# Attention over selected key blocks and a two-layer GELU: other products in the second layer, and one score scheme for all batches

## The chip, the cores and the metric

The kernel runs on one core of one Trainium2 chip. The metric is the device time of one execution in microseconds. Of 8 executions the median was 269.89 us (268.59 to 277.04). One execution was profiled: it took 270.17 us, of which the span from the first to the last instruction is 268.5 us, at a mean granted TensorE clock of 0.991.

A core has five engines, each with its own queue that runs in order: TensorE (PE), VectorE (DVE), ScalarE (ACT), GpSimd (POOL) and SyncE (SP, which here only issues transfers). TensorE multiplies a stationary operand, loaded first (PEld), with a moving one, and adds into PSUM. DVE and ACT read PSUM; all but TensorE write SBUF.

## The reference

There are 4 batches, 8 heads, 768 positions and 64 channels a head. Keys are taken in 12 blocks of 64. Each query scores the mean key of each block (the gate), keeps its top 3 causal blocks and its own block, and attends to those positions that are not after it.

```python
k_rep = k.reshape(B, H, n_blocks, block, D).mean(axis=3)
gate_scores = np.einsum('bhsd,bhnd->bhsn', q, k_rep)
causal = pos[:, None] // block >= np.arange(n_blocks)[None, :]
gate_scores = np.where(causal, gate_scores, -1000000000.0)
top_idx = np.argsort(gate_scores, axis=-1)[..., -top_k:]
...
sel = set(top_idx[b, h, i].tolist()) | {own_block[i]}
...
mask = mask & (pos[:, None] >= pos[None, :])
scores = np.where(mask, scale * np.matmul(q, k.transpose(0, 1, 3, 2)), -1000000000.0)
attn = softmax(scores)
attn_out = np.matmul(attn, v)
```

The heads of a token are laid side by side as x, 3072 rows of 512. Two layers follow, with `w_in` 512 by 2048 and `w_out` 2048 by 512:

```python
h = x @ w_in
g = gelu_tanh(h)
out = g @ w_out
```

Inputs and output are in fp32; the kernel multiplies in fp16.

## The kernel before

**Order of the work.** The code does not issue its instructions directly. `add(...)` records an operation: the engines that may run it with an estimated time on each, what it depends on, a priority, and the buffers that it takes and gives back. `Plan.solve` (lines 53 to 129) runs a list schedule over these estimates, picks an engine where there is a choice, hands out PSUM and other buffers, and sorts the operations by planned start. The instructions are then issued in that order, so each engine's queue is the planned one. On the chip a late operation holds up those behind it on its engine.

PSUM is shared in two groups (line 221). Two tiles `wide` of two banks each serve the scores and the first layer. Four tiles `bank` of one bank each serve `pre` (gates, transposes; at most 3), `pv` (sums of probabilities times values; at most 2) and `ops` (second layer; at most 2, in the last batch all 4).

**Stages.** Work goes by batch, and within a batch by pair `p` of heads (4 pairs a batch, 16 in all; `hp` is the pair within its batch and `i = p % 4` the set of buffers).

- `pre(p)` turns q and k so that channels lie on partitions, both heads above one another (rows 0 to 63 and 64 to 127), casts them to fp16, computes gates on TensorE and the choice of blocks on DVE, and lays the choice out as a mask of 12 rows a head. Batch 0 turns by TensorE; batches 1 to 3 by DVE (L418), from loads in 32 by 32 blocks.
- Scores come with keys on partitions and queries as columns, so that the exponentials are already the stationary operand of the product with the values. Only key chunks that are not after the queries are computed.
- The exponential is one ACT instruction a unit; GpSimd zeroes the half of the diagonal chunks that is after the query (affine select); the product with the values carries a column of ones that gives the sum of the row; DVE normalises (`norm2`, `norm`) and `turn_out` transposes the result into xT.
- `s1(b)` is the first layer with the GELU on ACT (L938, L950). Its result G is held in four quarters, A11, A12, A21, A22: even or odd chunk of 128 hidden units, first or second half of the batch's queries.
- `s2_plain(0)` is the second layer of batch 0 as it stands (L1025). `s2(b)` for batches 1 to 3 uses seven products of quarters in place of eight. The second layer of a batch is interleaved by the plan with the attention of the next batch.

**Two score schemes.** In batch 0, `heads2` (lines 674 to 783) works on both heads at once. A unit is a list of (key chunk, first query, number of queries). For each part, four matmuls are issued: q and k of head 0 on rows 0 to 63, of head 1 on rows 64 to 127, then the mask `mT2` against the constant `E2` in the same way, added into the same columns. Each uses 64 of TensorE's 128 rows. A unit has up to 512 columns a head. The data live in `kT2`, `qT2` and `mT2`, which lie inside the buffers `XS` of the second layer's sums; `E2` lies inside G.

In batches 1 to 3, `heads` (lines 845 to 922) works head by head. `kT16[i][h]` and `qT16[i][h]` hold 64 rows of data and, below them, 12 rows of mask and of the constant, so that one matmul of 76 rows gives masked scores. A unit is two key chunks, 896 columns, three matmuls (two in the last group). Two heads make six units a pair. The lower rows of `kT16` are filled once from E2 by eight small transfers on SP (`fill`, L375); the mask rows of `qT16` by copies from PSUM (batch 1) or from a transposing transfer into `mT` (batches 2 and 3).

**The second layer in seven products.** `FACT` (line 971) lists the two factors of each product. `w_sums` makes five sums of quarters of `w_out` (in two halves of the hidden units), `sums(b, c)` five sums of quarters of G for each of four chunks of a batch; three go to XS, two replace A21 and A12. `token(t)` (three a batch) runs the seven products into two banks, P and Q. Each `half` is one product: 8 matmuls of 256 columns into one half of a bank. P takes products 3 and 4, Q 1 and 6; both are copied out whole (ACT or DVE), DVE adds three times between the copied quarters (L1123), P takes 5 and 2 and is copied again, DVE subtracts it (L1138), and 7 is added at the end from Q (L1145).

Fillers (`warm`, L1174) are matmuls without use that the plan sets where TensorE would be idle.

Of the kernel before, what the change touches and what calls it, by code (L numbers as in the profile page):

```python
# [132 lines left out]
def kernel(  # L133
# [60 lines left out]
    for i in range(NK):  # L194
# [5 lines left out]
          for x in range(3)]  # L200
# [3 lines left out]
    kT2, qT2, mT2 = [[XS[x][:, 2 * i:2 * i + 2, :].rearrange("p a b -> p (a b)")  # L204
                      for i in range(HP)] for x in range(3)]
    E2 = G[:, 1, 1, NJ - 2:NJ, :].rearrange("p a b -> p (a b)")
# [5 lines left out]
    qT16, kT16, v16, madd = [], [], [], []  # L212
    for i in range(NB):
        qT16.append([persist.tile([128, S], FP16, name=f"qT_{i}_{h}")
                     for h in range(2)])
        kT16.append([persist.tile([128, S], FP16, name=f"kT_{i}_{h}")
                     for h in range(2)])
        v16.append(persist.tile([128, NC, 2, 65], FP16, name=f"v_{i}"))
        madd.append(persist.tile([128, NG, 64], FP16, name=f"madd_{i}"))
# [111 lines left out]
    def consts():  # L331
# [31 lines left out]
        for i in range(NB):  # L363
            def emit_p(_, i=i):
                nc.gpsimd.memset(v16[i][:, :, :, 64:65], 1.0)
                nc.gpsimd.memset(madd[i], 0.0)
                nc.gpsimd.memset(mT2[i][:, 0:128], 0.0)
                for h in range(2):
                    nc.gpsimd.memset(qT16[i][h][64:76, 0:128], 0.0)
            c_E["ones", i] = add({POOL: 1.1}, emit_p, [], prio=-45 + 10 * i)  # L370

    def fill(i):
        def emit(_):
            for h in range(2):
                nc.sync.dma_start(out=kT16[i][h][64:76, :], in_=E2[0:12])  # L375
        go = add({SP: 1.1}, emit, [c_E["E"], issued["v", 3]], 45 + i, lag=3.0)
        c_E["fill", i] = add({"NONE": 0.0}, lambda _: None, [go], 45)

    groups = [(0, 5), (1, 4), (2, 3)]
    last = {}  # L380

    def pre(p):
# [69 lines left out]
        else:  # L452
# [12 lines left out]
            def kc_all(h):  # L465
                def emit(eng):
                    copy(eng, kT16[i][h][0:64, :],
                         T["kT32", p][64 * h:64 * h + 64, :])
                return emit
            kcs = [add({DVE: 0.56, POOL: 0.85}, kc_all(h),  # L470
                       [t, old.get("k", None)], pr + 0.1) for h in range(2)]

# [104 lines left out]
        else:  # L577
            def q16(h):
                def emit(eng):
                    copy(eng, qT16[i][h][0:64, :],  # L580
                         T["qT32", p][h * 64:(h + 1) * 64, :])
                return emit
            q16s = [add({DVE: 0.56, ACT: 0.84}, q16(h), qcs + [old.get("s")],
                        pr + 0.1) for h in range(2)]
# [9 lines left out]
        def mask_dma(_):  # L594
            T["mT", p] = hd2.tile([128, S - 128], FP16, tag="mT",
                                 name=f"mT_{p}")
            nc.sync.dma_start_transpose(
                out=T["mT", p].rearrange("p (c q) -> p c q", q=128),
                in_=madd[i].rearrange("p g n -> p (g n)"))
# [19 lines left out]
        else:  # L619
            byPE = p < 2 * HP  # L620
            if byPE:
                m = add({PE: 0.3}, mask, [sel], pr, takes=("pre", ("mk", p, 0)))
            else:
                go = add({SP: 1.3}, mask_dma, [sel], -50)
                m = add({"DMA": 0.8}, lambda _: None, [go], pr, lag=6.0)

            def mc(h):
                def emit(eng):
                    src = (plan.buf["mk", p, 0].bitcast(FP16)[:, 128:S] if byPE
                           else T["mT", p])  # L630
                    copy(eng, qT16[i][h][64:76, 128:S],
                         src[64 * h:64 * h + 12, :])
                return emit
            mcs = [add({DVE: 0.5, ACT: 0.7} if byPE else {DVE: 0.33}, mc(h),
                       [m, old.get("s")], pr) for h in range(2)]
            if byPE:
                add({"NONE": 0.0}, lambda _: None, mcs, pr,
                    gives=[("mk", p, 0)])
            rdy[p] = [kcs[0::2] + [q16s[0], mcs[0], c_E["fill", i]],
                      kcs[1::2] + [q16s[1], mcs[1], c_E["fill", i]]]  # L640
# [33 lines left out]
    def heads2(p):  # L674
        i = p % NB
        base = 100 * p
        pvs = [[], []]
        for ui, unit in enumerate(units(p)):
# [4 lines left out]
            def st_e(_, u=u, unit=unit):  # L683
                st = plan.buf[("st",) + u]
                col = 0
                for jc, q0, w in unit:
                    for src, msk in ((kT2[i], False), (E2, True)):
                        mov = mT2[i] if msk else qT2[i]
                        for h in range(2):
                            nc.tensor.matmul(  # L690
                                st[:, 512 * h + col:512 * h + col + w],
                                src[64 * h:64 * h + 64,
                                    jc * 128:jc * 128 + 128],
                                mov[64 * h:64 * h + 64, q0:q0 + w],
                                start=not msk, stop=msk,
# [3 lines left out]
            st = add({PE: n * 2 / 2400 + 0.01}, st_e, rdy[p][late], pr,  # L699
                     takes=("wide", ("st",) + u))  # L700

            def ex_e(_, u=u, n=n):
# [8 lines left out]
                     [st, table(("exp", 0), [], base)], pr,  # L711
                     takes=("at", ("at", u)), gives=[("st",) + u])
            exps.setdefault(0, []).append(ex)
# [69 lines left out]
        last.setdefault(p, {}).update({"v": pvs[1][-1]})  # L783

    def norm(p, h):
        def emit(_):
            pvv = plan.buf["pv", p, h][:, 0:NC * 66].rearrange(
                "p (c w) -> p c w", w=66)
            if ("xn", p) not in T:
                T["xn", p] = hd.tile([128, NC, 2, 64], FP16, tag="xn",  # L790
                                     name=f"xn_{p}")
            zr = hd.tile([128, NC, 1], FP32, tag="zr", name=f"zr_{p}_{h}")
            nc.vector.reciprocal(out=zr, in_=pvv[:, :, 64:65])
            nc.vector.tensor_tensor(  # L794
                out=T["xn", p][:, :, h, :], in0=pvv[:, :, 0:64],
                in1=zr.to_broadcast([128, NC, 64]), op=ALU.mult)
        return emit

    def turn_out(p, norms, base):
# [28 lines left out]
        elif p == HP - 1:  # L828
# [15 lines left out]

    def heads(p):
        b, hp = divmod(p, HP)
        i = p % NB
        base = 1000 * b + 100 * hp
        norms = []
        for h in range(2):  # L850
            pvs = []
            for gi, (ja, jb) in enumerate(groups):
                u = (p, h, gi)
                pr = base + 10 * (3 * h + gi)
                wa = S - ja * 128
                wb = S - jb * 128

                def st_e(_, u=u, ja=ja, jb=jb, wa=wa, wb=wb, h=h):
                    st = plan.buf[("st",) + u]
                    for jc, cb in ((ja, 0), (jb, wa)):  # L860
                        s0 = jc * 128
                        w = S - s0
                        x = cb
                        while x < cb + w:
                            e = min(cb + w, (x // 512 + 1) * 512)
                            nc.tensor.matmul(  # L866
                                st[:, x:e], kT16[i][h][0:76, s0:s0 + 128],
                                qT16[i][h][0:76,
                                           s0 + (x - cb):s0 + (e - cb)],
                                start=True, stop=True)  # L870
                            x = e
                st = add({PE: 0.39}, st_e,
                         rdy[p][h] + [s1_mm[b - 1][2 * NJ - 2]], pr,
                         takes=("wide", ("st",) + u))

                def ex_e(_, u=u, n=wa + wb):
                    T["at", u] = atp.tile([128, 896], FP16, tag="at",
                                          name="at_%d_%d_%d" % u)
                    nc.scalar.activation(  # L879
                        out=T["at", u][:, 0:n],  # L880
                        in_=plan.buf[("st",) + u][:, 0:n],
                        func=AF.Exp, bias=0.0, scale=SCALE)
                ex = add({ACT: 0.84}, ex_e,
                         [st, table(("exp", b), list(gelus.get(b - 1, {}).values()), base)],
                         pr, takes=("at", ("at", u)),
                         gives=[("st",) + u])
                exps.setdefault(b, []).append(ex)

                def af_e(_, u=u, wa=wa):
                    at = T["at", u]  # L890
                    dg = bass.AP(at.tensor, at.offset,
                                 [at.ap[0], [wa, 2], [1, 128]])
                    nc.gpsimd.affine_select(  # L893
# [121 lines left out]
    def quads(x, diag):  # L1015
        return bass.AP(x.tensor, x.offset + (0 if diag else HD),
                       [x.ap[0], [3 * HD if diag else HD, 2], [1, HD]])
# [248 lines left out]
```

## Time and profile before

| what | us |
|---|---|
| median of 8 executions | 269.89 (268.59 to 277.04) |
| the profiled execution | 270.17 |
| its span | 268.5 |
| first layer, L938, 512 matmuls, busy | 85.2 |
| second layer with seven products, L1075, busy | 64.0 |
| second layer of batch 0, L1025, busy | 26.3 |
| scores of batches 1 to 3, L866, 192 matmuls, busy | 39.5 |
| scores of batch 0, L690, 192 matmuls, busy | 12.7 |
| probabilities times values, L905 and L754 | 27.3 and 8.6 |
| exponentials of batches 1 to 3, L879, 72 at 917 ns | 61.5 |
| exponentials of batch 0, L705, 24 at 917 ns | 21.4 |
| sums of quarters of G, L1009, 60 on DVE | 34.1 |
| sums of quarters of w_out, L991, 10 on DVE | 7.0 |

Busy times of matmuls overlap one another, since one starts before the one before it has ended; the distance from start to start says how long TensorE was taken. The stages lie one behind the other: attention of batch 0 up to 43.6 us, first layer of batch 0 to 65, attention of batch 1 with the second layer of batch 0 to 105.2, first layer of batch 1 to 127.9, attention of batch 2 with the second layer of batch 1 to 168.7, first layer of batch 2 to 191.4, attention of batch 3 with the second layer of batch 2 to 225.0, first layer of batch 3 to 245.7, and its second layer to the end.

### The profile page before, as it was taken

Reading aid. Unit: us, or ns where it says so; the run is one execution under the profiler, and the core shown is the slowest. Engines: PE = TensorE matmul, PEld = TensorE weight load, DVE = VectorE, ACT = ScalarE, POOL = GpSimd, SP = SyncE. Lnnn points to the kernel's source line nnn. Section 1 sums busy time; section 2 is a strip of 40 time slices with the busy share of each in tenths; the row PEclk is TensorE's granted clock in tenths of the full one; section 3 lists DMA queues with packets and bytes.
Section 4 is the critical chain, followed back from the end, with each engine's and each line's share of the span. In section 5 each row is a group of like instructions: output and inputs, shape, how many; then the busy total and the mean of one; then the engine's idle time right before and its main releaser. Section 6 shows DMA issues by size and latency. Waiting matters only on the chain.

```text
span 268.5 us, 6581 instructions
## 1 busy us (share of the span) xinstructions
PE 257.5 (96%) x2542; PEld 178.1 (66%) x2542; DVE 189.5 (71%) x554; ACT 173.6 (65%) x221; POOL 85.2 (32%) x165
## 2 busy tenths in 40 slices
PE   6999999999998999999897999999999999999993
PEld 5777777565555665555565788565777797567882
DVE  1777745713589999989998999999965463335532
ACT  2268688557968984667894975456799943665221
POOL 8557734001455461320283652020045400000000
PEclk9999999999999999999997999999999999999999
DMA  8996898999898969998894394231103312000222
GB/s 163 218 212 133 152 207 120 185 196 181 165 190 151 206 148 177 192 163 156 131 177 90 57 202 139 89 40 24 27 1 110 61 67 94 0 0 2 78 79 80
DMA packets 130816, 32.63 MB, mean 122 GB/s; under 512 B 124544, under 2 KB 126688, under 8 KB 130784
## 3 DMA queue, kind: packets, MB, share of 16 engines
q1 hardware_dynamic: 126048, 27.62, 51.4%
q0 software_dynamic: 3136, 4.19, 9.7%
q10 hardware_dynamic: 1600, 0.39, 0.7%
q8 instruction: 20, 0.33, 0.5%
q14 instruction: 12, 0.10, 0.1%
HBM read 27.26 MB, written 6.29 MB: 125 GB/s over the span
## 4 chain that ended last, share of the span: by engine, by line
PE 68%; DVE 17%; ACT 4%; SPq 3%; issue 2%; DMA 2%; POOL 2%; DVEq 0%; ACTq 0%; POOLq 0%
PE wide L938 23%; PE bank L1075 18%; PE wide L866 4%; PE wide L690 4%; PE bank L1174 3%; PE bank L1025 3%; PE bank L905 3%; ACT at L879 3%; DVE XS L1009 3%; SPq L263 2%; PE bank L754 2%; PE bank L398 2%; DVE qT L236 2%; PE bank L517 2%; DVE qT L418 2%
## 5 line engine op out<-in xcount | busy, mean ns | idle before, releaser
L938 PE MATMUL wide<-xT,w_in 128*128 128x384 f16 x512 | 85.2, 326 | 0.0
L950 ACT ACTIVATE G<-wide 128x768 f16<-128x768 f32 x64 | 51.9, 811 | 35.5 <-PE wide L938 35.0
L938 PEld LDWEIGHTS <-w_in 128*128 128x128 f16 x512 | 49.4, 98 | 33.4 <-issue 1.8
L879 ACT ACTIVATE at<-wide 128x896 f16<-128x896 f32 x72 | 61.5, 917 | 8.5 <-PE wide L866 4.6
L893 POOL TENSOR_SCALAR_AFFINE_SELECT at<-at 128x256 f16<-128x256 f16 x72 | 33.8, 473 | 61.4 <-ACT at L879 60.1
L866 PE MATMUL wide<-qT,kT 76*128 76x512 f16 (+1 forms) x192 | 39.5, 310 | 0.8 <-ACT at L879 0.7
L1075 PEld LDWEIGHTS <-G 128*128 128x128 f16 x288 | 27.6, 98 | 5.2 <-issue 1.0
L905 PEld LDWEIGHTS <-at 128*128 128x128 f16 x504 | 23.9, 99 | 10.5 <-POOL at L893 3.7
L1009 DVE TENSOR_TENSOR XS<-G 128x768 f16<-128x768 f16 x36 | 21.0, 619 | 13.7 <-ACT G L950 13.6
L905 PE MATMUL bank<-v,at 128*128 128x65 f16 x504 | 27.3, 197 | 2.5 <-DVE xn L794 1.8
L232 ACT COPY osb<-bank 128x512 f32<-128x512 f32 x23 | 13.5, 586 | 23.2 <-PE bank L1075 20.0
L705 ACT ACTIVATE at<-wide 128x1024 f16<-128x1024 f32 (+3 forms) x24 | 21.4, 917 | 9.2 <-PE wide L690 8.0
L1025 PE MATMUL bank<-w_out,G 128*128 128x512 f16 x96 | 26.3, 379 | 0.6 <-DVE xn L794 0.6
L866 PEld LDWEIGHTS <-kT 76*128 76x128 f16 x192 | 15.9, 99 | 11.0 <-issue 2.5
L1075 PEld LDWEIGHTS <-XS 128*128 128x128 f16 x216 | 20.5, 98 | 3.1
L234 POOL CAST v<-v_sd 128x768 f16<-128x768 f32 x13 | 11.8, 905 | 29.5 <-DMA v_sd<-in_v_dram 28.8
L234 POOL CAST kT<-kT 64x768 f16<-64x768 f32 x17 | 14.0, 822 | 21.9 <-DVE kT L418 21.6
L1075 PE MATMUL bank<-TS,G 128*128 128x256 f16 x144 | 20.4, 275 | 0.0
L1075 PE MATMUL bank<-w_out,G 128*128 128x256 f16 x144 | 19.8, 272 | 0.4 <-DVE w_out L991 0.4
L1075 PE MATMUL bank<-w_out,XS 128*128 128x256 f16 x144 | 19.5, 272 | 0.0
L1123 DVE TENSOR_TENSOR osb<-osb 128x256 f32<-128x256 f32 x27 | 11.7, 434 | 9.2 <-ACT osb L232 8.6
L418 DVE STREAM_TRANSPOSE kT<-k_sd 128x768 f32<-128x768 f32 x12 | 11.6, 970 | 6.1 <-DMA k_sd<-in_k_dram 6.0
(95 smaller groups left out, 345.7 us busy)
## 6 DMA issues: line engine op xcount, KB each, us to landing
out_dram<-osb SPq DMA_DIRECT2D x24, 256.0 KB
v_sd<-in_v_dram SPq DMA_DIRECT2D x26, 192.0 KB
k_sd<-in_k_dram SPq DMA_DIRECT2D x48, 96.0 KB
q_sd<-in_q_dram SPq DMA_DIRECT2D x48, 96.0 KB
w_in<-in_moe_w_in_dram POOLq DMA_DIRECT2D x2, 1024.0 KB, 11.4
w_out<-in_moe_w_out_dram POOLq DMA_DIRECT2D x2, 1024.0 KB, 12.3
G<-in_k_dram SPq DMA_DIRECT2D x4, 192.0 KB
G<-in_q_dram SPq DMA_DIRECT2D x4, 192.0 KB
```

Of the source, the lines that this page charges most:

```text
L234: nc.gpsimd.tensor_copy(out=out, in_=in_)
L418: nc.vector.transpose(out=T[key + "T32", p], in_=T[key, p].rearrange("p t j -> p (t j)"))
L705: nc.scalar.activation(out=T["at", u][:, :, 0:n], in_=plan.buf[("st",) + u].rearrange("p (h w) -> p h w", h=2)[:, :, 0:n], func=AF.Exp, bi ...
L866: nc.tensor.matmul(st[:, x:e], kT16[i][h][0:76, s0:s0 + 128], qT16[i][h][0:76, s0 + (x - cb):s0 + (e - cb)], start=True, stop=True)
L879: nc.scalar.activation(out=T["at", u][:, 0:n], in_=plan.buf[("st",) + u][:, 0:n], func=AF.Exp, bias=0.0, scale=SCALE)
L893: nc.gpsimd.affine_select(out=dg, in_=dg, compare_op=ALU.is_ge, fill=0.0, base=0, pattern=[[0, 2], [1, 128]], channel_multiplier=-1)
L905: nc.tensor.matmul(pvv[:, qc, 0:65], at[:, cb + (qc - jc) * 128: cb + (qc - jc + 1) * 128], v16[i][:, jc, h, :], start=(gi == 0 and jc == ...
L938: nc.tensor.matmul(hps[:, 512 * e:512 * e + HALF], w_in16[:, ci, (2 * j + e) * 128: (2 * j + e + 1) * 128], T["xT", b][:, ci, HALF * h:HAL ...
L950: nc.scalar.activation(out=G[:, :, h, j, :], in_=plan.buf["hps", b, j, h].rearrange("p (e w) -> p e w", e=2)[:, :, 0:HALF], func=AF.Gelu_a ...
L1009: nc.vector.tensor_tensor(out=dst[:, js], in0=i0[:, js], in1=i1[:, js], op=op)
L1025: nc.tensor.matmul(plan.buf["ops", b, ti], G[:, f % 2, 2 * ti // NC, f // 2, ti % (NC // 2) * 128:ti % (NC // 2) * 128 + 128], w_out16[:, ...
L1075: nc.tensor.matmul(dst[:, HD * h:HD * h + HD], FACT[m][0][:, j, t * 128:(t + 1) * 128], FACT[m][1][:, j, :], start=(first and j == 0 and h ...
```

## The change

**Scores.** `heads` and all that it needs go (`kT16`, `qT16`, `fill`, `norm`, `mT`). All batches use `heads2`. `kT2`, `qT2`, `mT2` become buffers of their own, one set for each `i`, and so does `E2`. In batches 1 to 3 the casts of q and k are one copy of 128 rows each instead of two of 64, with POOL allowed for q as well; the mask is one copy from PSUM in batch 1, and in batches 2 and 3 the transposing transfer writes `mT2` without a copy behind it. All of these wait for the last scores of the pair that used the buffers before.

Queries up to 191 have at most three causal blocks, so all of them are selected, and the first 64 queries of a diagonal chunk see their own block alone. The mask matmul of a part now starts at `max(q0, 192, jc * 128 + 64)`, and is left out where nothing remains. This holds in batch 0 too.

**Second layer.** The seven products are formed from four sums of each factor, each made from the one before. Products 1, 2 take raw quarters of both factors, 3 raw weights, 4 and 7 a raw or replaced quarter of G. One quarter of G is replaced instead of two, and one of `w_out`. In `token` the order is 1 and 5 into P, 2 and 6 into Q, 3 onto 5 in P, 4 over 1 in P, 7 onto 6 in Q. One half of a bank is copied; the other steps are DVE adds that read PSUM directly.

The last pair of every batch is turned by TensorE in two halves, as was done in batch 0 alone.

```diff
-    kT2, qT2, mT2 = [[XS[x][:, 2 * i:2 * i + 2, :].rearrange("p a b -> p (a b)")
-                      for i in range(HP)] for x in range(3)]
-    E2 = G[:, 1, 1, NJ - 2:NJ, :].rearrange("p a b -> p (a b)")
+    kT2, qT2, mT2 = [[persist.tile([128, S], FP16, name=f"{x}T2_{i}")
+                      for i in range(NB)] for x in "kqm"]
+    E2 = persist.tile([128, S], FP16, name="E2")
...
-            kcs = [add({DVE: 0.56, POOL: 0.85}, kc_all(h),
-                       [t, old.get("k", None)], pr + 0.1) for h in range(2)]
+            kcs = [add({DVE: 0.56, POOL: 0.85},
+                       lambda eng: copy(eng, kT2[i], T["kT32", p]),
+                       [t, old.get("s")], pr + 0.1)]
...
+            q16s = [add({DVE: 0.56, ACT: 0.84, POOL: 0.85},
+                        lambda eng: copy(eng, qT2[i], T["qT32", p]),
+                        qcs + [old.get("s")], pr + 0.1)]
...
-                go = add({SP: 1.3}, mask_dma, [sel], -50)
-                m = add({"DMA": 0.8}, lambda _: None, [go], pr, lag=6.0)
+                go = add({SP: 1.3}, mask_dma, [sel, old.get("s")], -50)
+                mcs = [add({"DMA": 0.8}, lambda _: None, [go], pr, lag=6.0)]
...
+                    q1 = max(q0, 192, jc * 128 + 64)
+                    for src, mov, lo in ((kT2[i], qT2[i], q0),
+                                         (E2, mT2[i], q1)):
+                        if lo >= q0 + w:
+                            continue
...
-            st = add({PE: n * 2 / 2400 + 0.01}, st_e, rdy[p][late], pr,
-                     takes=("wide", ("st",) + u))
+            cols = n + sum(max(0, q0 + w - max(q0, 192, jc * 128 + 64))
+                           for jc, q0, w in unit)
+            st = add({PE: cols / 2400 + 0.01}, st_e,
+                     rdy[p][late] + ([s1_mm[b - 1][2 * NJ - 2]] if b else []),
+                     pr, takes=("wide", ("st",) + u))
...
-    def heads(p):
...
-    FACT = {1: (XS[0], TS[:, 0]), 2: (XS[1], B11), 3: (A11, B12),
-            4: (A22, B21), 5: (XS[2], B22), 6: (A21, TS[:, 1]),
-            7: (A12, TS[:, 2])}
+    FACT = {1: (A11, B11), 2: (A12, B21), 3: (XS[2], B22),
+            4: (A22, TS[:, 2]), 5: (XS[0], TS[:, 0]), 6: (XS[1], TS[:, 1]),
+            7: (A21, B12)}
...
+                    (5, TS[:, 0], B12, B11, ALU.subtract),
+                    (6, TS[:, 1], B22, TS[:, 0], ALU.subtract),
+                    (7, B12, B22, B12, ALU.subtract),
+                    (4, TS[:, 2], B21, TS[:, 1], ALU.subtract)):
...
+                (5, XS[0], A21, A22, ALU.add),
+                (6, XS[1], XS[0], A11, ALU.subtract),
+                (3, XS[2], A12, XS[1], ALU.subtract),
+                (7, A21, A11, A21, ALU.subtract)):
...
+            half(1, "P", 1, True, [])
+            mm = half(5, "P", 0, False, [])
+            ao = add({DVE: 0.36, ACT: 0.4}, a_e, [mm], post,
+                     takes=("osb", ("osb", key)))
+            eo = add({DVE: 0.34}, join(
+                lambda: quad(3), lambda: two(bank_of("P")[:, 0:HD]),
+                lambda: quad(2)), [ao], post)
+            half(2, "Q", 0, True, [])
+            mm = half(6, "Q", 1, False, [])
+            bo = add({DVE: 0.61}, join(
+                lambda: quad(0, 2), lambda: two(bank_of("Q")),
+                lambda: quad(2).to_broadcast([128, 2, HD])), [mm, ao], post)
+            half(3, "P", 0, False, [eo])
+            mm = half(4, "P", 1, True, [])
+            co = add({DVE: 0.61}, join(
+                lambda: quad(1, 2), lambda: two(bank_of("P")),
+                lambda: quad(1, 2)), [mm, bo], post,
+                gives=[("ops", b, t, "P")])
+            mm = half(7, "Q", 1, False, [bo])
+            do = add({DVE: 0.61}, join(
+                lambda: quad(2, 2),
+                lambda: two(bank_of("Q")[:, HD:2 * HD]).to_broadcast(
+                    [128, 2, HD]),
+                lambda: quad(2, 2)), [mm, co], post,
+                gives=[("ops", b, t, "Q")])
...
-        heads(p)
+        heads2(p)
```

## The prediction

> **What bounds the kernel now.** I read the page's first two parts, then the table of stretches cut at the borders of the stages, then TensorE's order of time inside them, and last the costliest groups.
>
> ```profile
> PE 257.5 (96%) x2542; PEld 178.1 (66%) x2542; DVE 189.5 (71%) x554; ACT 173.6 (65%) x221; POOL 85.2 (32%) x165
> PEclk9999999999999999999997999999999999999999
> ...
> 65.00:105.20 40.20, 39.12 (x386) 22.01 (x384) 33.22 (x90) 32.11 (x41) 19.69 (x35) 1.00 0.90 172
> 127.90:168.70 40.80, 37.57 (x421) 29.39 (x419) 39.01 (x73) 29.95 (x38) 19.45 (x32) 0.96 0.67 131
> 191.40:225.00 33.60, 33.36 (x408) 27.16 (x406) 19.05 (x44) 26.60 (x34) 10.55 (x24) 1.00 0.18 51
> ```
>
> The columns of a stretch are its length, then the busy time of PE, PEld, DVE, ACT and POOL, then clock, DMA share and GB/s. The three stretches are the attention of batches 1, 2 and 3, each mixed with the second layer of the batch before. The same kind of work takes 40.2, 40.8 and 33.6 us. Busy PE is modelled, so I add up the work by steps from start to start: second layer 168 products of 256 columns at 0.109 (17.48 us for 160 in the chain) = 18.3; scores 24 units at 0.38 = 9.1; probabilities times values 168 at 0.031 = 5.2; the rest 0.3. That is 32.9 us. Batch 3's stretch is thus full of TensorE work to 0.7 us, batch 2's has 7.9 us of slack, and batch 1's, where the second layer is 96 products at 0.2165 = 20.8 and gates and transposes are 3.1, comes to 38.2 of 40.2: 2 us of slack. The first layer is 128 products in 20.80 us, all TensorE. So TensorE bounds nearly everything after 43 us; DVE is the second bound, at 39.0 of 40.8 us in batch 2's stretch.
>
> Where batch 2's slack lies:
>
> ```profile
> 128.69 0.60 PE L1174 MATMUL bank<-ident 128*128 128x256 f16 x4
> 129.13 0.55 PE L866 MATMUL wide<-qT,kT 76*128 76x512 f16 x3
> 129.51 1.26 PE L1174 MATMUL bank<-ident 128*128 128x256 f16 x10
> ...
> 133.10 0.38 PE L1075 MATMUL bank<-w_out,G 128*128 128x256 f16 x2 [0.45 <-DVE w_out L991]
> ...
> 143.12 0.79 PE L905 MATMUL bank<-v,at 128*128 128x65 f16 x21 [1.40 <-DVE xn L794]
> ```
>
> Fillers (L1174) run because the first product waits for weight sums at the end of DVE's queue; later the values' products wait for a normalisation (L794) that stands behind the sums (L991, L1009). After that gap the clock is 0.58 and 0.57 in the 4 us from 144 to 148, some 1.7 us more.
>
> **What the change costs TensorE.** Batches 1 to 3 leave the 76-row score matmuls (64 rows of data, 12 of mask) for the row halves that batch 0 has. One unit of each:
>
> ```profile
> 40.24 0.42 PE L754 MATMUL bank<-v,at 128*128 128x65 f16 x8
> 40.59 0.28 PE L690 MATMUL wide<-XS,XS 64*128 64x256 f16 x2
> 40.71 0.27 PE L690 MATMUL wide<-XS,G 64*128 64x256 f16 x2
> 40.82 0.27 PE L690 MATMUL wide<-XS,XS 64*128 64x256 f16 x2
> 40.92 0.27 PE L690 MATMUL wide<-XS,G 64*128 64x256 f16 x2
> 41.13 0.42 PE L754 MATMUL bank<-v,at 128*128 128x65 f16 x8
> ...
> 198.91 0.38 PE L905 MATMUL bank<-v,at 128*128 128x65 f16 x7
> 199.12 0.55 PE L866 MATMUL wide<-qT,kT 76*128 76x512 f16 x3
> 199.50 0.38 PE L1075 MATMUL bank<-w_out,XS 128*128 128x256 f16 x2
> ```
>
> Look at the starts. Two halves share 0.11 us, so they do run at once. But eight value products at 0.031 end at 40.49 and the halves start at 40.59; the last pair should be done at 41.03 and the next work starts at 41.13. About 0.10 us goes at each change between halves and full rows, 0.20 per unit. The old unit has none: 7 products in 0.21, 896 columns in 0.38, and on. [...]
>
> Scores per pair of heads, by steps seen in batch 0 (384 columns 0.16, 256 0.11, 128 0.055 for both halves). Data: 2 x 0.16 + 5 x 0.11 + 5 x 0.055 = 1.15. Masks, now 2,176 of 2,688 columns: 2 x 0.16 + 0.11 + 3 x 0.055 + 3 of 192 at 0.08 + 3 of 64. A pair of 64 columns is in no trace; it costs between half of 128 columns (0.027) and two value products of 65 columns (0.062); I take 0.045, in the middle. Masks 0.97, together 2.12 (2.06 to 2.17). Plus changes: six units, of which two stand together at a pair's start in about two of three cases, so 5.3 x 0.20 = 1.06 (5 x 0.19 to 6 x 0.20). New 3.18, old 6 x 0.38 = 2.28: **+0.90 a pair (+0.73 to +1.09), +3.6 a batch (2.9 to 4.4).** Value products stay 42 a pair.
>
> **What it takes from DVE, ACT and POOL.** Per pair one copy of 128 rows replaces two of 64: one cast of q (0.61 on DVE) and one of k (0.82 on POOL, 0.83 on DVE) fall away; of the mask copies two of 0.34 in batches 2 and 3, one of 0.51 in batch 1. Sums fall by 4 a batch at 0.57 to 0.62, weight sums by 2 at 0.7. Between 65 and 145 us, where DVE's queue is full, I count q 2.7 + k 1.7 + masks 4 + sums 2.4 + weight sums 1.4 = 12 us. The tail of a token keeps DVE level (5 adds, 0.42 + 3 x 0.7 with PSUM as a source, against 3 x 0.434 + 0.684 + 0.416) and spares ACT two of three copies of 0.59. The exponentials cost ACT 5 x 1.02 + 0.38 = 5.48 a pair, not 6 x 0.854 = 5.12; that 1.4 us a batch hides under 10 us of second layer left after the last pair of batch 3 (214.4 to 225). The first two products of a token now need one weight sum, the first of its chain, not the last two.
>
> **Moved waits.** The casts of k and q and, on SP, the mask transposes (L597) now wait for the last scores of four pairs before; these are done a stage earlier, so nothing behind them moves. The eight fills leave SP at 21.3 to 27.6 us; the next entry waits for a weight load until 35.5, so nothing is gained. The third product of P waits for a copy and an add of some 1.2 us after the second, covered by M2 and M6 (16 products, 1.75). Behind it on TensorE stand all later products and scores, so without that cover it would cost up to 1.2 us in each of nine tokens; I take 0. In the last layer the product with XS[0] needs the last sum 0.87 us after the layer starts instead of 1.75: 0.2 us late.
>
> **The sum.** Batch 0: mask columns shorten its units by 0.2 us a pair, and its stretch is a chain through ACT and DVE with filler on TensorE; -0.4 (-0.9 to +0.3). Batch 1: +3.6, less 1.0 of its 2 us of slack = +2.6 (0.9 to 4.4). Batch 2: +3.6, less 5.8 of its 7.9 (fillers 2.2, waits 2.1 and the low clock 1.5 go, the rest stays) = -2.2 (-5.0 to +2). Batch 3: +3.6, less nothing = +3.6 (2.7 to 4.9). Last layer +0.2 (-0.3 to 0.5). Together **+3.8 us**. The profiled execution took 270.17 (span 268.5), 0.28 above the median 269.89; so 274.0 on its own scale and **273.7** for the median.
>
> **Rivals.** *All slack is recovered* (chance 0.18): TensorE waits nowhere in batches 1 and 2: -0.4 + 1.6 - 4.3 + 3.6 + 0.2 = +0.7, 270.6. For it: DVE's 12 us exceed the waits. Against it: batch 1's waits are partly on loads and POOL, and two PSUM banks are now held by each pair's value sums beside two of the second layer, out of four. *Nothing is recovered* (0.16): 3 x 3.6 - 0.2 = +10.6, 280.5, if PSUM banks or the longer exponentials give new waits of the old size. *The change of mode hides* (0.14; the other side): if TensorE drains only when there is nothing to load ahead, the full queues of batches 1 to 3 take 64 x 0.20 = 12.7 us off: 261.0. It decides from 0.14 us per unit down, where 64 x 0.06 equals my +3.8. Against it: batch 0's drain stands behind back-to-back value products too, as in the lines above.
>
> **How the numbers follow.** The forecast has 0.52; its own range is 271.0 to 276.5. Runs can't tell less than 0.3% (0.8 us) from no change. Full recovery splits into slower 0.04, same 0.09, faster 0.05. Slower: 0.52 + 0.16 + 0.04 = 0.72; same 0.09; faster 0.14 + 0.05 = 0.19. The bounds of the terms add up to 267.3 and 282.0; the range, 266.5 to 280.5, leaves out the hidden change and a third of the case where nothing is recovered, 0.2 in all.
>
> **What would show it.** A 0.10 us step before and after each score unit in all batches, scores plus steps of 3.2 us a pair; batch 3's stretch at about 37 us, batch 2's at 38 to 39 with no filler and a clock of 1.00, DVE 20 us less in all. Wrong if batch 3's stretch stays under 35 us, or if batch 2's falls below 36.

## The result, and the profile after

The changed kernel takes 271.76 us (median of 11), the kernel before 269.52 beside it (32). The ratio is 1.0085 [1.0063, 1.0107]: slower by 0.85%. One execution of the changed kernel took 655.57 us and one of the kernel before 372.67, and the ratio is that of the ordinary ones. The forecast was 273.7 with a range of 266.5 to 280.5.

The profile shown here is of a further series of the changed kernel (272.16; 1.0084 [1.0054, 1.0114]). Its execution took 271.8 us with a span of 270.0, against 270.17 and 268.5 before, so the spans differ by 1.6 (270.04 and 268.46 with two decimals). The page's busy times, its clock, the first line of its chain and its score and value groups:

```profile
PE 263.7 (98%) x2926; PEld 179.8 (67%) x2926; DVE 165.4 (61%) x500; ACT 158.3 (59%) x196; POOL 72.3 (27%) x126
PEclk9999999999999999999999999999999999999999
...
PE 96%; DVE 2%; issue 0%; DVEq 0%
...
L658 PE MATMUL wide<-qT,kT 64*128 64x256 f16 (+2 forms) x384 | 43.1, 261 | 0.0
L658 PE MATMUL wide<-mT,E 64*128 64x128 f16 (+4 forms) x384 | 37.1, 238 | 0.0
L728 PE MATMUL bank<-v,at 128*128 128x65 f16 x672 | 33.4, 195 | 0.0
```

DVE has 24.1 us less to do, ACT 15.3, POOL 12.9; TensorE is busy 6.2 us longer and the slice of lower clock has gone. The last field of the three groups, idle time before them, is 0.0: TensorE no longer waits for anything at its scores and value products. The stretches of batches 1, 2 and 3, the second one up to where the first layer runs on (two of its matmuls run ahead, at 161):

```profile
65.30:108.10 42.80, 42.80 (x532) 23.59 (x530) 31.83 (x87) 28.80 (x36) 16.82 (x26) 1.00 0.89 172
130.40:169.00 38.60, 38.60 (x566) 29.48 (x566) 30.96 (x61) 25.58 (x30) 14.98 (x24) 1.00 0.70 138
190.00:226.70 36.70, 36.70 (x535) 28.50 (x535) 15.54 (x33) 26.25 (x32) 8.35 (x16) 1.00 0.25 46
```

In each of them the busy time of PE equals the length: no gap is left, though six fillers still run in batch 2's stretch. Batch 1's stretch is longer than before, batch 2's is shorter, batch 3's is longer again. The same table for all runs, cut where the first layer's matmuls start and end (worked out from their start times in each trace, without the two matmuls of batch 2's first layer that run 5 to 8 us ahead in six of these runs; the first layers of batches 0 and 3 take 21.9 and 20.6 in most of them and are left out):

| run | to the first layer of 0 | attention 1 | first layer 1 | attention 2 | first layer 2 | attention 3 | last layer, end |
|---|---|---|---|---|---|---|---|
| before | 42.9 | 41.1 | 21.7 | 41.7 | 21.7 | 33.8 | 23.0 |
| changed | 43.2 | 42.9 | 22.1 | 38.7 | 20.8 | 36.9 | 22.7 |
| layer_only | 42.2 | 41.1 | 21.7 | 38.7 | 21.2 | 33.2 | 22.7 |
| heads_only | 43.5 | 42.9 | 22.1 | 39.8 | 20.8 | 37.2 | 23.0 |
| layer_dve | 42.2 | 41.1 | 21.7 | 41.4 | 22.1 | 33.0 | 22.7 |
| beside | 43.2 | 44.4 | 22.1 | 40.1 | 20.8 | 38.3 | 22.7 |
| split | 43.2 | 48.7 | 22.1 | 44.6 | 20.8 | 42.7 | 22.7 |
| mask_full | 42.9 | 43.8 | 22.1 | 39.6 | 20.8 | 37.8 | 22.7 |

Changed less before, with two decimals: +0.34, +1.79, +0.37, -2.98, -0.84, +3.19 and -0.29, together +1.58.

### The profile page after: what moved, and what is told of

Its sections match the earlier page's. It is cut to its first block, busy times and chain, and to the rows that moved or that the text cites. A ratio compares the mean times of both kernels' runs of the same rounds, so it can differ in the third digit from the quotient of the medians.

```text
span 653.8 us, 7195 instructions
## 1 busy us (share of the span) xinstructions
PE 647.9 (99%) x2926; PEld 319.5 (49%) x2926; DVE 166.0 (25%) x500; ACT 161.0 (25%) x196; POOL 71.9 (11%) x126
## 4 chain that ended last, share of the span: by engine, by line
PE 99%; DVE 0%; issue 0%
PE wide L818 35%; PE bank L948 23%; PE wide L658 14%; PE bank L898 9%; PE bank L728 8%; PE bank L1046 3%; PE bank L383 2%; PE bank L498 2%; PE bank L771 1%; PE bank L386 1%; PE bank L566 1%; DVE osb L993 0%; DVE ident L180 0%; DVE ksb L196 0%; DVE bmask L187 0%
## 5 line engine op out<-in xcount | busy, mean ns | idle before, releaser
L818 PE MATMUL wide<-xT,w_in 128*128 128x384 f16 x512 | 230.1, 684 | 0.0
L818 PEld LDWEIGHTS <-w_in 128*128 128x128 f16 x512 | 88.7, 175 | 135.5 <-issue 134.6
L678 ACT ACTIVATE at<-wide 128x1024 f16<-128x1024 f32 x96 | 87.7, 917 | 163.6 <-PE wide L658 160.2
L658 PE MATMUL wide<-mT,E 64*128 64x128 f16 (+4 forms) x384 | 78.9, 437 | 0.0
L658 PE MATMUL wide<-qT,kT 64*128 64x256 f16 (+2 forms) x384 | 75.6, 417 | 0.0
L948 PE MATMUL bank<-w_out,G 128*128 128x256 f16 x216 | 71.0, 525 | 0.0
L705 POOL TENSOR_SCALAR_AFFINE_SELECT at<-at 128x256 f16<-128x256 f16 (+1 forms) x65 | 34.2, 528 | 279.6 <-ACT at L678 279.6
L728 PE MATMUL bank<-v,at 128*128 128x65 f16 x672 | 64.7, 279 | 0.0
L898 PE MATMUL bank<-w_out,G 128*128 128x512 f16 x96 | 60.6, 804 | 0.0
L948 PEld LDWEIGHTS <-G 128*128 128x128 f16 x288 | 44.6, 162 | 31.8 <-issue 4.8
L948 PE MATMUL bank<-TS,XS 128*128 128x256 f16 x144 | 48.4, 527 | 0.0
L1046 PE MATMUL bank<-ident 128*128 128x256 f16 x72 | 24.2, 495 | 2.1 <-DVE ident L180 2.1
```

Source lines behind the costliest of these rows:

```text
L658: nc.tensor.matmul(st[:, 512 * h + col + lo - q0: 512 * h + col + w], src[64 * h:64 * h + 64, jc * 128:jc * 128 + 128], mov[64 * h:64 * h ...
L678: nc.scalar.activation(out=T["at", u][:, :, 0:n], in_=plan.buf[("st",) + u].rearrange("p (h w) -> p h w", h=2)[:, :, 0:n], func=AF.Exp, bi ...
L705: nc.gpsimd.affine_select(out=dg, in_=dg, compare_op=ALU.is_ge, fill=0.0, base=0, pattern=pat, channel_multiplier=-1)
L728: nc.tensor.matmul(pvv[:, c, h, 0:65], at[:, h, col:col + 128], v16[i][:, jc, h, :], start=one, stop=False, skip_group_check=True)
L818: nc.tensor.matmul(hps[:, 512 * e:512 * e + HALF], w_in16[:, ci, (2 * j + e) * 128: (2 * j + e + 1) * 128], T["xT", b][:, ci, HALF * h:HAL ...
L898: nc.tensor.matmul(plan.buf["ops", b, ti], G[:, f % 2, 2 * ti // NC, f // 2, ti % (NC // 2) * 128:ti % (NC // 2) * 128 + 128], w_out16[:, ...
```

## The experiments

Ratios are to the kernel before, run beside each kernel on the same chip. Three chips were used, on which the kernel before took 269.92 (changed kernel again, layer_only, heads_only), 269.25 (beside, split, mask_full, plan_true) and 269.15 (the others), so medians from different chips are compared to some 0.8 us only; the profiled stretches say where a difference lies.

**The changed kernel again** is the measure for what follows.

> The changed kernel once more, for a profile of an ordinary execution and a closer time. Theory (score units in row halves cost TensorE about 0.9 us more a pair, and lighter DVE work gives batch 2's stretch its waits back): 271.8 us; the stretches of attention with second layer, which were 40.2, 40.8 and 33.6 us, come to about 42.8, 38.5 and 37. Rival (the new second layer is what costs time, through its adds from PSUM): the last layer and batch 3's stretch grow, with products of the second layer that wait for DVE, and batch 1's stretch, which has the old second layer, stays at 40.2.

Measured 272.16, 1.0084 [1.0054, 1.0114]. Where TensorE enters and leaves the halves shows in its order of time in batch 3's stretch:

```profile
195.64 0.41 PE L728 MATMUL bank<-v,at 128*128 128x65 f16 x8
195.99 0.34 PE L658 MATMUL wide<-qT,kT 64*128 64x384 f16 x2
196.16 0.33 PE L658 MATMUL wide<-mT,E 64*128 64x384 f16 x2
196.32 0.22 PE L658 MATMUL wide<-qT,kT 64*128 64x128 f16 x2
196.38 0.22 PE L658 MATMUL wide<-mT,E 64*128 64x128 f16 x2
196.53 0.61 PE L948 MATMUL bank<-w_out,XS 128*128 128x256 f16 x4
```

Eight value products at 0.031 are done at 195.89 and the halves start at 195.99; the last pair of 128 columns takes 0.055 from 196.38 and the next work starts at 196.53. That is 0.10 on each side, as in batch 0 before, though the queue is full. By such starts a pair's scores take 3.15 to 3.18 us in all, where they took 2.30.

**Each half of the change alone.** layer_only is the kernel before with the new second layer and the old scores of 76 rows; heads_only is the kernel before with the new scores and the old second layer.

```diff
# layer_only, of the diff above only
+    FACT = {1: (A11, B11), 2: (A12, B21), 3: (XS[2], B22),
+            4: (A22, TS[:, 2]), 5: (XS[0], TS[:, 0]), 6: (XS[1], TS[:, 1]),
+            7: (A21, B12)}
...
# heads_only, of the diff above only
-        heads(p)
+        heads2(p)
```

> The kernel before with the new second layer alone (four sums, new order of products), scores of batches 1 to 3 still by 76-row matmuls. Theory: TensorE's work is unchanged, DVE has some 4 us less before 145 us and the first product waits for no weight sum, so batch 2's stretch falls by 3 to 5 us and the others stay: 265 to 267 us. Rival (the new second layer costs time): 270 us or more.

> The kernel before with the score change alone, second layer as before. Theory: +3 to +3.6 us in batches 1 and 3 each, in batch 2 about as much less what 8 us of lighter DVE work gives back: 273 to 277 us, slower than both. Rival (the score change is the gain, since masks shrink and copies fall away): 269 us or less.

layer_only took 265.06, 0.9822 [0.9783, 0.986]; heads_only 273.31, 1.013 [1.0094, 1.0167]. So the second layer alone is a gain, the scores alone a loss, and **layer_only beats both kernels**. In spans the parts are worth -5.1 and +3.4, -1.6 in sum; together they gave +1.6. So 3.2 us of gain are claimed twice. The table shows where most of it lies: batch 2's attention and first layer fall by 3.6 with the layer alone and by 2.7 with the scores alone, but by 3.8 with both. The windows of batch 2's attention, layer_only first, then heads_only:

```profile
127.00:165.70 38.70, 37.17 (x448) 29.13 (x446) 37.57 (x70) 27.48 (x34) 19.34 (x34) 1.00 0.68 138
```

```profile
130.60:170.40 39.80, 39.72 (x567) 29.81 (x566) 35.86 (x79) 28.71 (x36) 17.87 (x26) 1.00 0.76 136
```

In layer_only TensorE still has 1.5 us of gaps and DVE is nearly full; in heads_only TensorE is full. Once TensorE is full in this stretch, DVE time that is saved buys nothing more there.

**Is it DVE's time that batch 2 gained?** layer_dve is layer_only with 14 sums more on DVE, as many as the old second layer had, into a tile that nothing reads.

```diff
+    spare = persist.tile([128, 1024], FP16, name="spare")
...
+            def more(_, js=js):
+                nc.vector.tensor_tensor(
+                    out=spare.rearrange("p (j t) -> p j t", j=NJ // 2),
+                    in0=B11[:, js], in1=B22[:, js], op=ALU.add)
+            add({DVE: 0.6}, more, [prev], 1600 + x)
...
+        def more(_):
+            nc.vector.tensor_tensor(
+                out=spare[:, 0:2 * HALF].rearrange("p (j t) -> p j t", j=2),
+                in0=A12[:, js], in1=A22[:, js], op=ALU.add)
+        add({DVE: 0.5}, more, [prev], 1000 * b + 600 + 4 * c)
```

> layer_only with the DVE work of the old sums put back: one sum more per chunk of G and one more per half of w_out, into a tile that nothing reads (14 DVE instructions, some 8 us, of which 3.8 fall before 145 us). Theory A (layer_only gains by less DVE work): it loses most of its gain again, 267.5 to 269. Theory B (it gains because the first products of a token wait for no late sum): the gain stays, 265 to 266.

It took 268.37, 0.9961 [0.9938, 0.9984]; in spans 3.4 of the 5.1 us that layer_only had gained are gone. The window of batch 2's attention, TensorE's waits in it, and the group of the added sums:

```profile
127.10:168.50 41.40, 39.06 (x441) 29.84 (x439) 38.78 (x85) 27.39 (x34) 19.13 (x33) 0.96 0.66 133
```

```profile
134.79 0.39 PE L1083 MATMUL bank<-TS,XS 128*128 128x256 f16 x2 [0.49 <-DVE XS L1015]
...
138.42 0.39 PE L1083 MATMUL bank<-TS,XS 128*128 128x256 f16 x2 [1.25 <-DVE XS L1015]
```

```profile
L1022 DVE TENSOR_TENSOR spare<-G 128x768 f16<-128x768 f16 x12 | 6.8, 563 | 0.0
```

The stretch is back to 41.4, the clock back to 0.96, and the second layer's products wait for sums (L1015), 1.7 us in two waits; in the kernel before, its value products had waited 1.8 for normalisations and its second layer 0.4 for a weight sum. So batch 2's gain is DVE's length of queue, and a part of it comes by way of the clock: after the wait of 1.25 the clock is 0.85, 0.50 and 0.80 in the three stretches of 2 us from 138 to 144, some 1.7 us. Three of layer_dve's ten executions had a mean clock of 1.00 and took 266.88, 266.91 and 267.98; the other seven, at 0.990 to 0.994, took 268.33 to 268.64. One thing is left open: with 14 operations more the plan also sets another order, and no run holds the order fixed. The 1.7 us that stay are in other places: 0.7 ahead of the first layer of batch 0, 0.8 in batch 3's attention, 0.3 at the end, less 0.1 left over in batch 2.

**What does a change of mode cost?** A change of mode is one between the row halves and full rows. Both kernels put the same 72 small full-row matmuls (64 columns) into the score units of batches 1 to 3 of the changed kernel, and the scores overwrite what they write. beside has them at the head of a unit, so they add themselves only; split has them between the parts of a unit, so that the halves are left and entered again.

```diff
# beside
+                for x in range(1, len(unit) if p >= HP else 0):
+                    nc.tensor.matmul(st[:, 128 * x:128 * x + 64], ident16,
+                                     ident16[:, 0:64], start=True,
+                                     stop=True, skip_group_check=True)
...
# split
-                for jc, q0, w in unit:
+                for x, (jc, q0, w) in enumerate(unit):
+                    if x and p >= HP:
+                        nc.tensor.matmul(st[:, col:col + 64], ident16,
+                                         ident16[:, 0:64], start=True,
+                                         stop=True, skip_group_check=True)
```

> The changed kernel with 72 small matmuls more (64 columns, full rows, 6 a pair in batches 1 to 3) at the head of each score unit, next to other full-row work; the scores overwrite what they write. Both theories: 72 x 0.03 = 2 us more than the changed kernel, about 274.

> The same 72 matmuls, but between the parts of a score unit, so that each makes TensorE leave the row halves and come back. Theory (each change between halves and full rows costs 0.10 us of TensorE): 72 x 0.19 = 13.7 us more than with the matmuls beside, about 288. Rival (the gap at the edge of a unit is another wait, or hides in full queues): the same as beside, about 274.

beside took 275.88, 1.0239 [1.0196, 1.0282]; split 289.15, 1.0729 [1.0683, 1.0775]. They differ by 13.27 us. By the traces TensorE enters the halves 45 times a batch in split, 24 times in beside and 21 times in the changed kernel, so split has 63 round trips more than beside in three batches: **0.21 us for leaving and entering once**. The steps give 0.19 between other work and 0.20 at the inserted matmuls. The expected 13.7, 72 round trips at 0.19, was thus met in part by luck: fewer round trips at a higher price. A unit of the same shape in beside and in split:

```profile
202.92 0.22 PE L662 MATMUL wide<-mT,E 64*128 64x128 f16 x2
203.07 0.20 PE L652 MATMUL wide<-ident 128*128 128x64 f16 x1
203.21 0.28 PE L662 MATMUL wide<-qT,kT 64*128 64x256 f16 x2
203.33 0.24 PE L662 MATMUL wide<-mT,E 64*128 64x192 f16 x2
203.41 0.27 PE L662 MATMUL wide<-qT,kT 64*128 64x256 f16 x2
203.52 0.25 PE L662 MATMUL wide<-mT,E 64*128 64x192 f16 x2
```

```profile
203.72 0.28 PE L662 MATMUL wide<-qT,kT 64*128 64x256 f16 x2
203.84 0.25 PE L662 MATMUL wide<-mT,E 64*128 64x192 f16 x2
204.02 0.20 PE L653 MATMUL wide<-ident 128*128 128x64 f16 x1
204.16 0.28 PE L662 MATMUL wide<-qT,kT 64*128 64x256 f16 x2
204.28 0.25 PE L662 MATMUL wide<-mT,E 64*128 64x192 f16 x2
```

From one mask to the next data pair it is 0.08 in beside and 0.32 in split. beside itself is 4.1 longer than the changed kernel in spans, where 72 matmuls at 0.03 make 2.2. The first two lines of its fence show where the rest comes from: here the added matmul stands between two units that had stood together, and 0.29 pass from pair to pair instead of 0.055. There are 3 such places a batch, 9 in all, 1.7 to 1.9 us.

**The masks.** mask_full gives batches 1 to 3 their mask matmuls over all queries again.

```diff
+                nc.gpsimd.memset(mT2[i][:, 0:128], 0.0)
...
-                    q1 = max(q0, 192, jc * 128 + 64)
+                    q1 = max(q0, 192, jc * 128 + 64) if p < HP else q0
```

> The changed kernel with mask matmuls over all queries of each part in batches 1 to 3, as batch 0 had before. Theory (TensorE sets the pace, so columns count): 512 columns a pair more for both halves, 0.24 us by the steps seen, 12 x 0.24 = 2.9 us more than the changed kernel, 274.5 to 275. Rival (the changes of mode set the pace, and columns hide): no difference, 272.

Measured 274.35, 1.0184 [1.014, 1.0228]: 2.2 us over the changed kernel in medians and in spans, where 2.9 were expected. In the table each of the three attentions is 0.85 longer: 512 columns a pair at 0.16 per 384 are 0.21 a pair, not the 0.24 expected, and 0.85 a batch. The sum isn't 2.6, since the time to the first layer of batch 0 fell by 0.4, although batch 0's masks are the same: the plan, with the zeroing added on POOL, came out in another order. So the trimming is worth 0.85 a batch in a stretch that is full.

**What the plan is told.** plan_true adds the change of mode to the plan's estimate of a unit.

```diff
-            st = add({PE: cols / 2400 + 0.01}, st_e,
+            st = add({PE: cols / 2400 + (0.2 if p >= HP else 0.01)}, st_e,
```

> The changed kernel, with the list schedule told 0.2 us per score unit instead of 0.01 in batches 1 to 3. Theory (TensorE has no idle time left in these stretches): within 0.8 us of the changed kernel, 271.3 to 272.9. Rival (the loss is an order planned with too short scores): 270 or less.

Measured 273.08, 1.0134 [1.0095, 1.0172], 0.9 over the changed kernel in medians and 1.7 in the profiled spans: 0.6 ahead of the first layer of batch 0, +0.5, -0.4 and +0.4 in the three attentions, +0.5 in batch 2's first layer. That is a little above the expected 271.3 to 272.9, and the intervals of the two ratios overlap. A truer estimate did not help. Why the order it leads to is worse was not followed up.

**Can layer_only be made better?** layer_trim0 takes the shorter masks into its batch 0; layer_share lets POOL cast q and ACT copy masks, to take work from DVE.

```diff
# layer_trim0, in the mask matmuls of batch 0
+                    q1 = max(q0, 192, jc * 128 + 64)
+                    for src, mov, lo in ((kT2[i], qT2[i], q0),
+                                         (E2, mT2[i], q1)):
...
# layer_share
-            q16s = [add({DVE: 0.56, ACT: 0.84}, q16(h), qcs + [old.get("s")],
+            q16s = [add({DVE: 0.56, ACT: 0.84, POOL: 0.85}, q16(h), qcs + [old.get("s")],
...
-            mcs = [add({DVE: 0.5, ACT: 0.7} if byPE else {DVE: 0.33}, mc(h),
+            mcs = [add({DVE: 0.5, ACT: 0.7} if byPE else {DVE: 0.33, ACT: 0.75}, mc(h),
```

> layer_only with the mask matmuls of batch 0 cut to queries past 191. Theory (batch 0 is a chain through ACT and DVE with filler on TensorE, and its score units lie on that chain): 0 to 0.8 us less than layer_only, 264.3 to 265.1. Rival (no effect, or a plan that comes out worse): 265 to 266.

> layer_only where the list schedule may also put the casts of q on POOL and the copies of the transposed masks on ACT. Theory (what is left of slack in batch 2's stretch, 38.5 us for 32.9 us of TensorE work, is DVE's queue): 1 to 3 us less than layer_only, 262 to 264. Rival (POOL and ACT get late with their own work, affine selects and exponentials): 265 us or more.

layer_trim0 took 264.56, 0.9827 [0.9797, 0.9857], which can't be told from layer_only; the time to batch 0's first layer is 42.23 in both. layer_share took 265.99, 0.9886 [0.9859, 0.9913], 0.9 more than layer_only in medians and 1.5 in the profiled spans. It is shorter by 0.4 in batch 3's attention and by 0.6 in batch 1's, but longer by 0.9 in batch 1's first layer, 0.7 in batch 2's attention, 0.4 ahead of batch 0's first layer and 0.3 in that layer: DVE is busy 6.8 us less and POOL 11.9 us more, and the time came back as delays elsewhere.

## Why the prediction was right, and where it was off

**The side and the reason held.** TensorE bounds the kernel, the new scores cost it time in every unit, and the saved time of the other engines pays that back only where TensorE had waited. 271.76 lies in the forecast's own range of 271.0 to 276.5, 1.9 below its point; 0.4 of that comes from the kernel before, which took 269.52 in this series and not 269.89.

**The cost of the scores held.** Forecast: 3.18 a pair and +0.90; measured 3.15 to 3.18 and +0.85 to +0.88. The change of mode was put at 0.20 a unit and 5.3 times a pair; by split and beside it is 0.21, by the steps 0.19, and the trace has 21 entries a batch, 5.25 a pair. The pair of 64 columns, put at 0.045 in the middle of its bounds, is at the lower one. TensorE's order of time at the head of batch 2's stretch:

```profile
130.46 0.28 PE L658 MATMUL wide<-qT,kT 64*128 64x256 f16 x2
130.58 0.19 PE L658 MATMUL wide<-mT,E 64*128 64x64 f16 x2
130.61 0.22 PE L658 MATMUL wide<-qT,kT 64*128 64x128 f16 x2
```

From the mask's start to the next is 0.03, about half of the 0.055 of 128 columns: this short pair cost its columns, no more. The rival in which the change of mode hides has fallen: each side of a unit takes the same 0.10 in the full queue of batch 3 as in batch 0. The prediction calls that time a drain; the runs show its length and not what TensorE does in it.

**Batch 3: +3.2, forecast +3.6.** No slack to recover, so the cost of four pairs stands there nearly bare. heads_only has it too (+3.4), layer_only not (-0.5).

**Batches 1 and 2: the term that was mis-sized.** I let 1.0 of batch 1's 2 us of slack and 5.8 of batch 2's 7.9 come back, 6.8 in all, and held that "the rest stays". With 3.5 of cost a batch, batch 1's attention came out at +1.8, so 1.7 came back; batch 2's attention with the first layers around it, between which two matmuls have moved, at -3.4, so 6.9 came back: 8.6 in all. What stays is eight fillers at 0.109, 0.9 us (L1046, two in the first layer of batch 1 and six in batch 2's attention). That makes 9.5 against the 9.9 that I had counted: the slack was sized rightly, the share that is recovered was not. TensorE without a wait is what the rival "all slack is recovered" asked for, and its sum was +0.7; the 0.9 of fillers is what lies between it and the measured +1.6, while the misses in batch 0, batch 3 and the last layer nearly cancel. So the measured time lies in the forecast's own range without being nearer to it than to that rival: +1.6 in spans is closer to the rival's +0.7 than to +3.8, and +2.2 in medians lies midway. The mechanism in these two batches is closer to the rival.

Why so much came back in batch 2: the queue of DVE got shorter by more than the instructions that I took out of it. DVE's order of time before, then POOL's in the same stretch, then DVE's after:

```profile
130.41 0.56 DVE L1009 TENSOR_TENSOR G<-G 128x768 f16<-128x768 f16 x1
...
131.48 0.76 DVE L1009 TENSOR_TENSOR XS<-G 128x768 f16<-128x768 f16 x1
...
132.98 0.75 DVE L1009 TENSOR_TENSOR XS<-G 128x768 f16<-128x768 f16 x1
...
136.75 0.55 DVE L1009 TENSOR_TENSOR G<-G 128x768 f16<-128x768 f16 x1
...
145.31 0.55 DVE L1009 TENSOR_TENSOR G<-G 128x768 f16<-128x768 f16 x1
```

```profile
131.28 0.56 POOL L893 TENSOR_SCALAR_AFFINE_SELECT at<-at 128x256 f16<-128x256 f16 x1 [10.49 <-ACT at L879]
132.08 0.43 POOL L893 TENSOR_SCALAR_AFFINE_SELECT at<-at 128x256 f16<-128x256 f16 x1 [0.25 <-ACT at L879]
132.89 0.43 POOL L893 TENSOR_SCALAR_AFFINE_SELECT at<-at 128x256 f16<-128x256 f16 x1 [0.38 <-ACT at L879]
...
136.78 0.78 POOL L893 TENSOR_SCALAR_AFFINE_SELECT at<-at 128x256 f16<-128x256 f16 x1 [0.37 <-ACT at L879]
```

```profile
130.35 0.55 DVE L886 TENSOR_TENSOR XS<-G,XS 128x768 f16<-128x768 f16 x1
...
132.69 0.55 DVE L886 TENSOR_TENSOR G<-G 128x768 f16<-128x768 f16 x1
...
135.18 0.65 DVE L886 TENSOR_TENSOR G<-G 128x768 f16<-128x768 f16 x1
...
137.07 0.20 DVE L748 RECIPROCAL zr<-bank 128x6 f32<-128x6 f32 x1 [0.35 <-PE bank L728]
```

The same sum takes 0.55 alone and 0.75 when it begins while a select of POOL is running (131.48, 132.98). The one at 136.75 began 0.03 before a select and kept its 0.55; there the select took 0.78 in place of 0.41. Over the whole execution 15 of the 60 sums before overlapped POOL's work by more than 0.05, at 0.74 in the mean against 0.55; after, 4 of 48 at 0.59. That is 15 x 0.19 = 2.9 us on DVE before and 0.2 after, which my count did not have. The last sum of this stretch began at 145.31 before; now it begins at 135.18, and at 137.07 DVE waits for TensorE and not the other way round. That the shorter queue is the cause is what layer_dve shows, but for the plan's order; how much of it the overlap alone is worth was not tried. Elsewhere the count held: DVE has 24.1 us less, where 20 were forecast, and the four adds of a token's tail, counted as five, are level at 22.4 us against 21.6.

**Batch 0: +0.3, forecast -0.4.** The trimmed masks are worth nothing there: layer_trim0 has them and its stretch is the same to 0.01. The stretch is 42.2 in layer_only, layer_dve and layer_trim0, 42.7 in layer_share, 43.5 in heads_only and 43.2 in the changed kernel. In mask_full, which differs from the changed kernel in batch 0 by some zeroing on POOL alone, it is 42.9, and in plan_true, where only an estimate for the other batches differs, 43.8. So the plan's order moves it by 0.4 to 0.6; which operation does it is open.

**Last layer: -0.3, forecast +0.2.** layer_only has the same -0.3 and heads_only none, so it belongs to the new second layer.

In order of time the misses are +0.7, -0.8, -1.2, -0.4 and -0.5: forecast +3.8 less 2.2 is the measured +1.6.

## What to carry to other kernels

Count the changes between row tiles and full rows before packing two heads into halves: here the packed streaming of a pair (2.1 us) is no slower than the 76-row one (2.3), and some five round trips at 0.19 to 0.21 turn it into a loss. Two edits that each relieve the same queue don't add, so measure each alone: here one was a gain of 1.8% that the other one hid. To see what an edit costs the engine that bounds, look at a stretch in which that engine is full already, for there the cost shows bare.

## What the runs showed of the hardware

- Leaving and entering the row halves cost 0.19 us by the steps and 0.21 by split and beside, in full queues too; the rival in which it hides needed less than 0.14.
- Where a DVE sum and a GpSimd select or cast ran at the same time, the one that began second took longer. In the kernel before, the eight sums of quarters of G that began during a select took 0.75 to 0.76 and the two that began during a cast of v 1.17 and 1.18, against 0.55 alone; five such sums that began first took 0.55 to 0.56, and selects that began during a sum, of quarters of G or of w_out, took up to 0.86 in place of 0.41. The loss was in each of these cases what the first one had still to run, less some 0.14: 0.34 left and 0.20 lost, 0.77 left and 0.63 lost; for a select 0.51 left and 0.37 lost. What the second one waits for, no run shows.
- A data pair of 128 columns and a mask pair of 64 in the halves took 0.055 and 0.03 in the changed kernel, each matmul with a weight load of its own (2,926 of each): half the columns took about half the time.
